# One product in 32 of the attention backward moved from VectorE to GpSimd by way of a ScalarE copy, and its group of units turned wholly by the DMA crossbar

## The chip, the cores and the metric

The kernel runs on one core of one Trainium2 chip. The metric is device time in microseconds. Before the change the median of three runs is 2561.26 us (2560.20 to 2564.32). The engines are TensorE (PE in the profile; its weight loads are PEld), VectorE (DVE), ScalarE (ACT), GpSimd (POOL) and SyncE (SP), which issues DMA. Matrix products land in PSUM, from which VectorE and ScalarE read.

## The reference

One transformer block (adaLN modulation, multi-head softmax attention, an MLP with squared ReLU) is computed forward and backward; the outputs are the block's result and the gradients of nine inputs. The sequence has S = 2048 tokens of width D = 512, with H = 32 heads of DH = 16. The change lies in the backward of the attention. For each head, with P the softmax probabilities, it computes

```
S  = Q K^T * scale            (2048 x 2048)
P  = exp(S), normalised       (the normalisation is folded into padded rows of V and dO)
dP = dO V^T - rowwise term    (2048 x 2048, one product of TensorE)
dS = P * dP                   (elementwise)
dV = P^T dO,  dK = dS^T Q,  dQ = dS K
```

The first four lines have 32 x 2048 x 2048 elements each, and the elementwise work on them is what occupies ScalarE (exp) and VectorE (P * dP).

## The kernel before, in words

The backward of the attention is `attn_bwd`. It loops over eight groups `g` of four heads, two head pairs `jp` in each, four chunks `c` of 512 keys, and sixteen blocks `ib` of 128 queries. One value of (g, jp, c, ib) is a **unit**: two heads `a`, 128 queries by 512 keys each. Four units in a row (`G = 4`, index `i`) are a **group**; a chunk has four groups. There are 1024 units, 256 groups and 64 chunks.

The order of instructions on every engine is the order in which the Python emits them; nothing reorders them. In each iteration, for each head `a`:

- PE computes the scores of this unit into an `st` tile (line 1555), and then `dP` of the *previous* unit into a `dp` tile (line 1494).
- ScalarE takes the exponential of the scores into `pu`, bf16 (line 1559).
- VectorE multiplies `dp` in PSUM by `pu` and writes `ds`, bf16 (line 1496). `ds` is one tile for the four units of a group.

`st` and `dp` come from rings of three PSUM buffers each (lines 1348 and 1349), `pu` from six buffers, `ds` from three, and the turned `dsT` from four. An instruction that writes a buffer waits until its reader of three tiles before is done.

After the two heads, work on older units follows on PE. In odd iterations `kv` (line 1448) multiplies `ds` and `pu` of two units, four and five units back, into the accumulator `acckv`; at the end of a chunk of keys (`ib` = 15) ScalarE copies `acckv` to `kvT` (line 1451). Since `kv` runs a group late, that copy falls into the last iteration of group 0 of the following chunk. In even iterations `dq` (line 1470) multiplies turned blocks of dS, `dsT`, by K.

`dsT` is made in two ways. In iteration 2 of a group, `turn_ds` has PE turn the four 128x128 blocks of the group's first product (i = 0, a = 0) into an `st` tile (line 1513), and ScalarE copies them into `dsT[:, 0:4]` (line 1514). The other 28 blocks are turned by one transposing DMA on SP's queue, issued in `dS` when the group's last unit is done (line 1504). `dq` reads `dsT` two groups later.

At the first and second group after the end of a head pair, `turn` (line 1459) has PE turn eight blocks of `kvT`, with two short copies by ScalarE to `dk_t` and `dv_t` (line 1463), and VectorE copies the accumulated dQ out (line 1477).

GpSimd's queue holds loads for the next head pair or group of heads. At the start of most groups it runs a one-element copy `tick` (line 1543), which waits for the first product of the group before, and then issues one DMA (line 1544).

`junk6` and `csq` are two f32 tiles of 128x512 in SBUF; the backward of the attention does not use them until its end.

Of the kernel before, what the change touches and what calls it, by code (L numbers as in the profile page):

```python
# [12 lines left out]
ALU = mybir.AluOpType  # L13
# [6 lines left out]
P = 128  # L20
# [85 lines left out]
class K:  # L106
# [1315 lines left out]
    def attn_bwd(self):  # L1422
# [7 lines left out]
        tc, nc = self.tc, self.nc  # L1430
        S, D, H, NQ, ST, SC = self.S, self.D, self.H, self.NQ, self.ST, self.SC
        G = 4
# [20 lines left out]
        def turn(g, jp, kvT, s0):  # L1453

            h0 = 4 * g + 2 * jp
            n = ST // 2
            tp = stp.tile([P, n, P], BF16, name="st")
            for st in range(n):
                nc.tensor.transpose(tp[:, st, :], kvT[:, (s0 + st) * P:(s0 + st + 1) * P], self.ident[:])
            v = tp[:].rearrange("p s (t a e) -> p t s a e", t=2, a=2)  # L1460
            for t, dst in enumerate((self.dk_t, self.dv_t)):
                d = dst[:, s0:s0 + n, h0 * DH:(h0 + 2) * DH].rearrange("p s (a d) -> p s a d", a=2)
                nc.scalar.copy(d, v[:, t, :, :, 0:DH])

        def dq(u, heads):
            (T, g, jp, c, ib, i, dsT) = u
            for a in heads:
                col = (2 * jp + a) * DH
                for sub in range(4):
                    nc.tensor.matmul(accq[:, ib, a, :], lhsT=dsT[:, (i * 2 + a) * 4 + sub, :],  # L1470
                                     rhs=T["K"][:, 4 * c + sub, col:col + DH],
                                     start=(c == 0 and ib == 0 and a == 0 and sub == 0), stop=False,
                                     skip_group_check=True)
            if c == SC - 1 and ib == ST - 1 and 1 in heads:
                h0 = 4 * g + 2 * jp
                d = self.dq_t[:, :, h0 * DH:(h0 + 2) * DH].rearrange("p s (a d) -> p s a d", a=2)
                nc.vector.tensor_scalar(d, accq[:], self.scale, None, ALU.mult)

        def kv_two(n=2):
            for u in pend[2 - n:2]:  # L1480
                kv(u)
            (T, g, jp, c, ib, kvT, pu, ds) = pend[1]
            del pend[:2]
            if c % 2 and ib == ST - 1 and (g, jp) == (NQ - 1, 1):
                turnq.append((g, jp, kvT, 4 * (c - 1)))
            elif c == SC - 1 and ib == ST - 1:
                turnq.extend((g, jp, kvT, s0) for s0 in (0, ST // 2))

        def dP(u, a):

            (T, g, jp, c, ib, kvT, pu, dsg, i, grp) = u
            rd = slice(64 - 64 * jp, 128 - 64 * jp)
            dp = dpp.tile([P, 512], F32, name="dp")
            nc.tensor.matmul(dp[:], lhsT=T["dOT"][rd, ib * P:(ib + 1) * P],  # L1494
                             rhs=masked["VT"][2 * jp + a][rd, 512 * c:512 * (c + 1)], start=True, stop=True)
            nc.vector.tensor_tensor(dsg[:, i, a], dp[:], pu[:, a, :], ALU.mult)  # L1496

        def dS(u):

            (T, g, jp, c, ib, kvT, pu, dsg, i, grp) = u  # L1500
            pend.append((T, g, jp, c, ib, kvT, pu, dsg[:, i]))
            if i == G - 1:
                dsT = grp[0]
                nc.sync.dma_start_transpose(dsT[:, 4:, :], dsg[:].rearrange("p i a k -> p (i a k)")[:, 512:])
                for i in range(G):
                    pendq.append((T, g, jp, c, ib - G + 1 + i, i, dsT))

        def turn_ds(dsg, grp):

            dsT = dtp.tile([P, 8 * G, P], BF16, name="dsT")  # L1510
            tp = stp.tile([P, 4, P], BF16, name="st")
            for b in range(4):
                nc.tensor.transpose(tp[:, b, :], dsg[:, 0, 0, b * P:(b + 1) * P], self.ident[:])  # L1513
            nc.scalar.copy(dsT[:, 0:4, :], tp[:])  # L1514
            grp.append(dsT)

        tick = self.tick
        T = self.T0
        turnq, last = [], None
        for g in range(NQ):  # L1520
            for jp in range(2):
                if jp == 0:
                    if g + 1 < NQ:
                        Tn, later = self.load_group(g + 1)
                    else:
                        Tn, later = None, self.wq_pieces(1) + self.load_wmt()
                    cut = len(later) // 2 if Tn else len(later)
                    pieces = self.pair_pieces(g, 1) + later[:cut]
                    later = later[cut:]
                elif g + 1 < NQ:  # L1530
                    pieces = self.pair_pieces(g + 1, 0) + later
                else:
                    pieces = [(self.xhat1_6[:, st, :], self.xhat1_d.rearrange("(st p) d -> p st d", p=P)[:, st, :])
                              for st in range(ST)]
                kvT = kvp.tile([P, S], BF16, name="kvT")
                total = len(pieces)
                for c in range(SC):
                    c0 = 512 * c
                    for ib0 in range(0, ST, G):
                        m = c * (ST // G) + ib0 // G  # L1540
                        while pieces and (total - len(pieces)) * SC * ST <= m * G * total:
                            if last:
                                nc.gpsimd.tensor_copy(tick[:], last[7][0:1, 0, 0, 0:1])  # L1543
                            nc.gpsimd.dma_start(*pieces.pop(0))
                        dsg, grp = self.dsp.tile([P, G, 2, 512], BF16, name="ds"), []
                        for i in range(G):
                            ib = ib0 + i
                            q = slice(ib * P, (ib + 1) * P)
                            if turnq and i == 2:
                                turn(*turnq.pop(0))  # L1550
                            pu = self.pup.tile([P, 2, 512], BF16, name="pu")
                            for a in range(2):
                                stt = stp.tile([P, 512], F32, name="st")
                                rs = slice(64 * jp, 64 * jp + 64)
                                nc.tensor.matmul(stt[:], lhsT=T["QT"][rs, q], rhs=masked["KT"][2 * jp + a][rs, c0:c0 + 512],  # L1555
                                                 start=True, stop=True)
                                if last:
                                    dP(last, a)
                                nc.scalar.activation(pu[:, a, :], stt[:], ACT.Exp, scale=self.scale)  # L1559
                            if last:  # L1560
                                dS(last)
                            last = (T, g, jp, c, ib, kvT, pu, dsg, i, grp)
                            if i % 2 == 1 and len(pend) >= 4:
                                kv_two()
                            elif i % 2 == 0 and len(pendq) > 2 * G:
                                for _ in range(4 if len(pendq) > 3 * G else 2):
                                    dq(pendq.pop(0), [0, 1])
                            if i == 2:
                                turn_ds(dsg, grp)
            T = Tn  # L1570
        with tc.manual_schedule(engines=ALL):
            for t in (2, 0):
# [338 lines left out]
```

The softmax here doesn't subtract the row's maximum and nothing guards it: scores larger than these inputs give would overflow.

## Time and profile before

| | |
|---|---|
| median of 3 runs | 2561.26 us |
| span of the profiled execution | 2562.0 us |
| its own time beside the span | no more than the span is shown for it; 0.7 us over the median |
| attention backward, first to last P * dP | 1180.6 to 2437.0 us |
| PE busy in the span | 2483.2 us (97%) |
| ScalarE busy | 2314.2 us (90%) |
| VectorE busy | 1767.4 us (69%), nearly all of the backward's stretch |
| GpSimd busy | 569.5 us (22%) |
| transposing DMAs of dS | 256, 6.7 us from issue to landing (median) |

How to read it: an engine's share is a mean over stages. Before 1180 us VectorE is busy two or three tenths, after it nine. A row of a group gives the busy time, the mean duration of one instruction in ns, and after the bar the idle time just before them with what ended it. Durations on ScalarE and VectorE overlap a little: the next instruction starts before the last one's recorded end, so the distance between starts is what one costs. Two heads' matmuls run beside each other on different rows of the array, so PE's records overlap too.

### The profile page before, as it was taken

Reading aid. Unit: us, or ns where it says so; the run is one execution under the profiler, and the core shown is the slowest. Engines: PE = TensorE matmul, PEld = TensorE weight load, DVE = VectorE, ACT = ScalarE, POOL = GpSimd, SP = SyncE. Lnnn points to the kernel's source line nnn. Section 1 sums busy time; section 2 is a strip of 40 time slices with the busy share of each in tenths; the row PEclk is TensorE's granted clock in tenths of the full one; section 3 lists DMA queues with packets and bytes.
Section 4 is the critical chain, followed back from the end, with each engine's and each line's share of the span. In section 5 each row is a group of like instructions: output and inputs, shape, how many; then the busy total and the mean of one; then the engine's idle time right before and its main releaser. Section 6 shows DMA issues by size and latency. Waiting matters only on the chain.

```text
span 2562.0 us, 77852 instructions
## 1 busy us (share of the span) xinstructions
PE 2483.2 (97%) x31239; PEld 1227.4 (48%) x31239; DVE 1767.4 (69%) x3651; ACT 2314.2 (90%) x3757; POOL 569.5 (22%) x1137
## 2 busy tenths in 40 slices
PE   8999899999999999899999999999999999999998
PEld 4555555555555554663444444444444444444443
DVE  6222323323322344667999999999999999999957
ACT  7999999999999996436999999999999999999935
POOL 3554521320221131353011111111111111111223
PEclk9999999999999999999999999999999999999999
DMA  4588742450351153799999999999999999999997
GB/s 165 118 180 196 173 95 83 100 113 22 112 128 49 39 143 113 154 190 211 205 205 202 199 200 201 203 204 200 197 199 198 208 201 197 201 201 229 213 202 191
DMA packets 1193040, 425.37 MB, mean 166 GB/s; under 512 B 1138004, under 2 KB 1161686, under 8 KB 1192678
## 3 DMA queue, kind: packets, MB, share of 16 engines
q1 hardware_dynamic: 1153542, 319.25, 64.2%
q0 software_dynamic: 37056, 100.11, 13.1%
q8 instruction: 244, 4.00, 0.6%
q10 hardware_dynamic: 2080, 1.05, 0.1%
q14 instruction: 118, 0.97, 0.1%
HBM read 73.73 MB, written 62.40 MB: 53 GB/s over the span
## 4 chain that ended last, share of the span: by engine, by line
PE 67%; ACT 20%; DMA 5%; issue 4%; POOL 2%; DVE 1%; SPq 1%; POOLq 0%; DVEq 0%; ACTq 0%
PE st L1555 20%; ACT pu L391 16%; PE acckv L1448 11%; PE accq L1470 8%; PE st L388 7%; PE accbank L322 3%; PE dp L1494 3%; ACT pu L1559 2%; PE st L1513 2%; PE dps L1047 2%; PE pps L1234 2%; PE dp L1604 1%; PE st L1699 1%; DMA dsT<-ds 1%; DMA ev_tm<-ev_fm 1%
## 5 line engine op out<-in xcount | busy, mean ns | idle before, releaser
L1496 DVE TENSOR_TENSOR ds<-dp,pu 128x512 bf16<-128x512 f32 x2048 | 1236.2, 679 | 13.1 <-PE dp L1494 10.2
L1559 ACT ACTIVATE pu<-st 128x512 bf16<-128x512 f32 x2048 | 1073.7, 612 | 46.4 <-PE dp L1494 22.5
L391 ACT ACTIVATE pu<-st 128x1024 bf16<-128x1024 f32 x992 | 912.1, 1077 | 4.6 <-PE st L388 4.4
L388 PE MATMUL st<-QTm,KTq 128*128 128x512 bf16 x1984 | 588.6, 377 | 19.5 <-ACT pu L391 6.0
L322 PEld LDWEIGHTS <-pu 128*128 128x128 bf16 x8192 | 347.5, 96 | 236.1 <-issue 3.1
L322 PE MATMUL accbank<-Vaug,pu 128*128 128x17 bf16 x8192 | 357.7, 171 | 1.2 <-ACT Vaug L522 0.9
L1494 PE MATMUL dp<-m,q 64*128 64x512 bf16 x1024 | 345.7, 382 | 1.1 <-DVE g2w L1053 0.7
L1494 PE MATMUL dp<-m,dOTg 64*128 64x512 bf16 x1024 | 344.6, 381 | 0.1
L1470 PEld LDWEIGHTS <-dsT 128*128 128x128 bf16 x8192 | 239.5, 96 | 213.8 <-issue 209.7
L1555 PE MATMUL st<-m,q 64*128 64x512 bf16 x1024 | 319.5, 382 | 9.2 <-ACT pu L1559 7.5
L1555 PE MATMUL st<-m,QTg 64*128 64x512 bf16 x1024 | 318.9, 381 | 9.5 <-ACT pu L1559 7.8
L388 PEld LDWEIGHTS <-KTq 128*128 128x128 bf16 x1984 | 188.3, 96 | 176.9 <-issue 125.5
L1543 POOL COPY tick<-ds 1x1 bf16<-1x1 bf16 x223 | 39.6, 178 | 1005.4 <-DVE ds L1496 1005.4
L1448 PE MATMUL acckv<-ds,q 128*16 128x512 bf16 x1024 | 154.0, 381 | 0.0
L1448 PE MATMUL acckv<-pu,dOg 128*16 128x512 bf16 x1024 | 154.0, 381 | 0.0
L1448 PE MATMUL acckv<-ds,Qg 128*16 128x512 bf16 x1024 | 154.0, 381 | 0.0
L1448 PE MATMUL acckv<-pu,q 128*16 128x512 bf16 x1024 | 154.0, 381 | 0.0
L1514 ACT COPY dsT<-st 128x512 bf16<-128x512 bf16 x256 | 152.4, 595 | 1.0 <-PE st L1513 1.0
L1470 PE MATMUL accq<-Kg,dsT 128*128 128x16 bf16 x4096 | 143.3, 170 | 3.4 <-DMA dsT<-ds 3.4
L1470 PE MATMUL accq<-q,dsT 128*128 128x16 bf16 x4096 | 143.6, 170 | 0.4 <-DMA dsT<-ds 0.3
L302 POOL DMA_DIRECT2D QTm<-QTq_d x124 | 63.3, 512 | 341.3 <-PE st L388 320.2
L329 DVE RECIPROCAL rl<-accbank 128x4 f32<-128x4 f32 x128 | 22.9, 179 | 162.6 <-PE accbank L322 162.5
(379 smaller groups left out, 2864.8 us busy)
## 6 DMA issues: line engine op xcount, KB each, us to landing
KTq<-KTq_d POOLq DMA_DIRECT2D x24, 512.0 KB, 3.9
duT_d<-auT POOLq DMA_DIRECT2D x3, 1792.0 KB, 7.8
aT_d<-rT POOLq DMA_DIRECT2D x3, 1792.0 KB, 11.1
KTq_d<-KTq SPq DMA_DIRECT2D x32, 128.0 KB, 2.0
QTq_d<-ev_fm SPq DMA_DIRECT2D x32, 128.0 KB, 3.9
VTq_d<-vT POOLq DMA_DIRECT2D x4, 1024.0 KB, 6.8
dsT<-ds SPq DMA_TRANSPOSE x256, 6.7
dx<-dx_d SPq DMA_DIRECT2D x16, 256.0 KB, 4.4
```

What stands on the lines that cost most here:

```text
L302: nc.gpsimd.dma_start(QTm[j][32 * j:32 * j + 32, :], self.QTq_d[g, 32 * j:32 * j + 32, 512 * qc:512 * (qc + 1)])
L322: nc.tensor.matmul(acc[:, a, sub, :], lhsT=pu[:, a, sub * P:(sub + 1) * P], rhs=Vaug[:, kb, h, :], start=(kb == 0 and a == 0 and sub == 0) ...
L388: nc.tensor.matmul(stt[:, a, :], lhsT=KT[:, kb * P:(kb + 1) * P], rhs=QTm[2 * jp + a][:], start=True, stop=True)
L391: nc.scalar.activation(pu[:], stt[:], ACT.Exp, scale=self.scale)
L1047: nc.tensor.matmul(pt[:], lhsT=a[st], rhs=g_tm[:, st, :], start=(st == 0), stop=(st == ST - 1))
L1448: nc.tensor.matmul(acckv[r:r + DH, :], lhsT=T[n][:, ib, col:col + DH], rhs=src[:, a, :], start=(ib == 0), stop=(ib == ST - 1))
L1470: nc.tensor.matmul(accq[:, ib, a, :], lhsT=dsT[:, (i * 2 + a) * 4 + sub, :], rhs=T["K"][:, 4 * c + sub, col:col + DH], start=(c == 0 and i ...
L1494: nc.tensor.matmul(dp[:], lhsT=T["dOT"][rd, ib * P:(ib + 1) * P], rhs=masked["VT"][2 * jp + a][rd, 512 * c:512 * (c + 1)], start=True, sto ...
L1496: nc.vector.tensor_tensor(dsg[:, i, a], dp[:], pu[:, a, :], ALU.mult)
L1514: nc.scalar.copy(dsT[:, 0:4, :], tp[:])
L1555: nc.tensor.matmul(stt[:], lhsT=T["QT"][rs, q], rhs=masked["KT"][2 * jp + a][rs, c0:c0 + 512], start=True, stop=True)
L1559: nc.scalar.activation(pu[:, a, :], stt[:], ACT.Exp, scale=self.scale)
```

## The change

In group 1 of every chunk (`off(c, ib)`: units 4 to 7), the dP tile of the group's first unit and second head is no longer multiplied by VectorE. ScalarE copies it from PSUM to `junk6` or `csq`, in turn, right after the exponential of the following unit's second head, and GpSimd multiplies the copy by `pu` and writes the same part of `ds`. In the same group `turn_ds` only allocates `dsT`; PE turns nothing, ScalarE copies nothing to `dsT`, and the transposing DMA takes all 32 blocks. That is 64 of 2048 tiles and 64 of 256 groups. The other groups are unchanged. (c * SC + ib // G) % 4 is ib // 4, since SC is 4.

```diff
             nc.tensor.matmul(dp[:], lhsT=T["dOT"][rd, ib * P:(ib + 1) * P],
                              rhs=masked["VT"][2 * jp + a][rd, 512 * c:512 * (c + 1)], start=True, stop=True)
+            if a == 1 and i == 0 and off(c, ib):
+                return dp
             nc.vector.tensor_tensor(dsg[:, i, a], dp[:], pu[:, a, :], ALU.mult)
+
+        def off(c, ib):
+            return (c * SC + ib // G) % 4 == 1
+
+        def dP_pool(u, dp):
+            (T, g, jp, c, ib, kvT, pu, dsg, i, grp) = u
+            f = (self.junk6, self.csq)[(c * SC + ib // G) // 4 % 2]
+            nc.scalar.copy(f[:], dp[:])
+            nc.gpsimd.tensor_tensor(dsg[:, i, 1], f[:], pu[:, 1, :], ALU.mult)
...
             if i == G - 1:
-                dsT = grp[0]
-                nc.sync.dma_start_transpose(dsT[:, 4:, :], dsg[:].rearrange("p i a k -> p (i a k)")[:, 512:])
+                dsT, n = grp
+                nc.sync.dma_start_transpose(dsT[:, n:, :], dsg[:].rearrange("p i a k -> p (i a k)")[:, n * P:])
...
-        def turn_ds(dsg, grp):
+        def turn_ds(dsg, grp, skip):
             dsT = dtp.tile([P, 8 * G, P], BF16, name="dsT")
+            grp.extend((dsT, 0 if skip else 4))
+            if skip:
+                return
             tp = stp.tile([P, 4, P], BF16, name="st")
             for b in range(4):
                 nc.tensor.transpose(tp[:, b, :], dsg[:, 0, 0, b * P:(b + 1) * P], self.ident[:])
             nc.scalar.copy(dsT[:, 0:4, :], tp[:])
-            grp.append(dsT)
...
-                                if last:
-                                    dP(last, a)
+                                held = dP(last, a) if last else None
                                 nc.scalar.activation(pu[:, a, :], stt[:], ACT.Exp, scale=self.scale)
+                                if held is not None:
+                                    dP_pool(last, held)
...
                             if i == 2:
-                                turn_ds(dsg, grp)
+                                turn_ds(dsg, grp, off(c, ib))
```

## The prediction

> **What bounds the kernel now.** I read the page's groups first, then the busy time by stage, then the timeline of one chunk, then single instructions on VectorE. The change touches only the attention backward, 1180 to 2437 us: 64 chunks (one per head pair and 512 keys) of four groups of four units. I write (n,a) for unit n of a chunk (0 to 15) and head a. The changed group is group 1, units 4 to 7: its product (4,1) moves, and its four turns on TensorE go.
>
> ```profile
> L1496 DVE TENSOR_TENSOR ds<-dp,pu 128x512 bf16<-128x512 f32 x2048 | 1236.2, 679 | 13.1 <-PE dp L1494 10.2
> L1559 ACT ACTIVATE pu<-st 128x512 bf16<-128x512 f32 x2048 | 1073.7, 612 | 46.4 <-PE dp L1494 22.5
> L1514 ACT COPY dsT<-st 128x512 bf16<-128x512 bf16 x256 | 152.4, 595 | 1.0 <-PE st L1513 1.0
> ```
>
> VectorE works 1236 of these 1257 us on one instruction, with 13 us idle in front of it. Its ends overlap: by single starts (1717.08, 1718.28 below, two apart) one costs 0.598 us of its queue, eight a group are 4.79 us. That looks like the bound. By stage:
>
> ```profile
> 1400.00:1700.00 300.00, 295.42 (x4214) 127.47 (x4213) 296.69 (x493) 292.60 (x582) 37.08 (x106) 1.00 1.02 201
> ```
>
> PE is busy 295, VectorE 297, ScalarE 293 of 300 us, GpSimd 37: three engines close together, so the order inside a chunk decides. Columns here are start, duration, engine:
>
> ```profile
> 1713.17 0.70 ACT L1451 ACTIVATE kvT<-acckv,kvs 128x512 bf16<-128x512 f32 x1
> 1713.74 3.07 ACT L1559 ACTIVATE pu<-st 128x512 bf16<-128x512 f32 x6
> ...
> 1714.41 0.37 PE L1555 MATMUL st<-m,QTg 64*128 64x512 bf16 x1 [0.25 <-ACT pu L1559]
> 1714.42 0.39 PE L1494 MATMUL dp<-m,dOTg 64*128 64x512 bf16 x1
> ...
> 1715.28 0.39 PE L1494 MATMUL dp<-m,dOTg 64*128 64x512 bf16 x1
> ...
> 1716.23 0.38 PE L1513 MATMUL st<-ident,ds 128*128 128x128 bf16 x4
> ...
> 1716.55 0.39 PE L1494 MATMUL dp<-m,dOTg 64*128 64x512 bf16 x1
> 1716.67 0.62 ACT L1514 COPY dsT<-st 128x512 bf16<-128x512 bf16 x1
> 1716.86 0.37 PE L1555 MATMUL st<-m,QTg 64*128 64x512 bf16 x1
> ...
> 1717.14 4.23 ACT L1559 ACTIVATE pu<-st 128x512 bf16<-128x512 f32 x8
> ...
> 1717.73 0.39 PE L1494 MATMUL dp<-m,dOTg 64*128 64x512 bf16 x1
> ```
>
> The reader is to see that this is group 1 and that it comes right behind the chunk's extra ScalarE work, the kvT copy: the six exponentials (4,0) to (6,1) start late, PE idles 0.25 us for one of them, and from there ScalarE has no gap. The dp rows shown are (4,1), (5,0), (6,0), (7,0). Now VectorE's products of (5,0), (6,0), (7,0), then (9,1), each asked for alone; and a case where VectorE really stood idle for its dp, with that dp:
>
> ```profile
> 1715.83 0.68 DVE L1496 TENSOR_TENSOR ds<-dp,pu 128x512 bf16<-128x512 f32 x1
> 1717.08 0.69 DVE L1496 TENSOR_TENSOR ds<-dp,pu 128x512 bf16<-128x512 f32 x1
> 1718.28 0.68 DVE L1496 TENSOR_TENSOR ds<-dp,pu 128x512 bf16<-128x512 f32 x1
> ...
> 1721.27 0.68 DVE L1496 TENSOR_TENSOR ds<-dp,pu 128x512 bf16<-128x512 f32 x1
> ```
> ```profile
> 1420.75 0.39 PE L1494 MATMUL dp<-m,dOTg 64*128 64x512 bf16 x1
> ...
> 1421.28 5.14 DVE L1496 TENSOR_TENSOR ds<-dp,pu 128x512 bf16<-128x512 f32 x8 [0.45 <-PE dp L1494]
> ```
>
> From dp's start to the product at the earliest is 0.53 us. In group 1 the distances are 0.55, 0.53 and 0.55: VectorE is "busy", but it has nothing waiting. At (9,1) the distance is 1.06 (dp 1720.21): there dp tiles wait, and VectorE sets the pace. So VectorE binds in groups 2, 3 and 0; in group 1 ScalarE and PE bind. The product that is removed lies in group 1. That is what my forecast rests on.
>
> **The change, part by part.**
>
> *Removed: one VectorE product per changed group.* 64 x 0.598 = 38.3 us of VectorE. It counts only if (5,0) can start earlier. Its dp starts at 1715.28, behind st(5,1), which waited for ScalarE (1714.41), so (5,0) starts at 1715.80 at best, 0.03 before now. The rest becomes idle VectorE.
>
> *Added and moved on ScalarE.* The copy of dp(4,1) to f stands behind exp (5,1) and ahead of exp (6,0); the dsT copy behind exp (6,1) goes. Copies of 128x512 f32 out of PSUM to f32 last 572 to 588 ns in the later stages, the dsT copy 595: the exchange is even, nine instructions before and after. Exponentials in this stretch follow each other by 0.48. Hence f starts at 1715.18 + 0.48 = 1715.66 (dp(4,1) is ready by 1714.9) and ends about 1716.25; exp (6,0) starts at 1716.13 instead of 1715.70, (6,1) at 1716.61, and (7,0), with no copy ahead of it, at 1717.09 (now 1717.14). Bounds for the slot of f: 0.45 (a 572 ns copy less the 0.12 of overlap) and 0.57 (the kvT copy, 1713.17 to 1713.74); I take 0.47 to 0.48, the dsT copy's. A buffer's next user starts 0.05 after its release (below, 1716.81 to 1716.86), so f frees dp(4,1)'s buffer at 1716.30, where VectorE freed it at 1715.96; dp(6,0) is the next user.
>
> *Removed on PE.* Four turns, 0.32 us from 1716.23 to the next st at 1716.55, and their st tile out of a ring of three. So st(7,0) goes at 1716.23, dp(6,0) at 1716.30 (now 1716.55). st(7,1) today waits for the end of exp (6,1), 1716.81 (hence 1716.86), because the turns' tile sits in the ring. Then it waits for exp (6,0), which f has pushed to end at 1716.74: st(7,1) at 1716.79. The gain on the path is 0.07 us. Behind it stand kv and dp(7,0), now at 1717.73, then 1717.66: earliest product 1718.19. VectorE's own queue: (5,0) 1715.80 and four more by 0.598 gives (7,0) at 1718.19. Both say 0.09 sooner than 1718.28. PE works without a gap to (9,1), which waits for VectorE again: the 0.09 is kept, no more is added, and what is late next is again ScalarE in the next group 1.
>
> *Chunks that open a head pair* (15 of the 64) carry eight kvT turns and two ScalarE copies in group 1, and VectorE idles there already (0.45 us, shown). The timeline from 1417 to 1426 shows a ScalarE hole of 0.1 us before those copies and a spacing of 0.27 between them, so f pushes exp (6,0) by 0.23 only, to 1421.62, end 1422.23. st(7,1) goes at 1422.28 instead of 1422.54; PE is gapless from there to the product (9,0), which idles 0.19 us for dp today. Gain 0.26.
>
> *Added on GpSimd.* One product of f by P, 64 times. Nearest rows: f32 by f32 1283 ns, bf16 by bf16 1163. It runs 1716.4 to 1717.7. It is first read by kv of unit 4, four units later, at 1719.32: 1.6 us of cover, and the transposing DMA is later still. Behind it in the queue stands the next group's tick and load, now at 1715.45, then about 1717.7; the loads are for the next head pair or the next group of heads and one head pair (16 of them in 1257 us, so 79 us) spreads 12 to 16 of them, so nobody waits. Exp (10,0), six units on, reuses P's buffer, at 1720.28. Cost nothing; if the cover were gone, each us beyond 1.6 would stop PE 64 times.
>
> The Trainium skill (GPSIMD Engine Reference, 4.1 Engine selection) speaks against this move: elementwise work belongs on VectorE, GpSimd being about twice as slow for two inputs. The rows agree on the ratio (1.16 to 1.28 against 0.68 us); charged to the path the rule would add some 64 x 0.6 = 38 us, an estimate, charged to a cover of 1.6 us nothing.
>
> *Moved: four blocks to the crossbar.*
>
> ```profile
> L1504 SPq DMA_TRANSPOSE dsT<-ds x256: 3370/3624/6962, 1185.6 to 2440.0; - x128
> ```
>
> 28 blocks take 3.62 us of SP's queue, so 32 take 4.14, of a group of at least 4.2 (seven products). Landing takes 6.7 us, then about 7.2; dq reads the tile two groups (9.5 us) after the issue, and VectorE rewrites ds sixteen products (9.6) after. Cost nothing. The DMA engines rest about 0.9 us of each group now (half-us stretches from 1700.5 show 0.12 and 0.00 of their share), which covers the 0.5.
>
> *Sum.* 49 x 0.08 + 15 x 0.26 = 3.9 + 3.9 = 7.8 us (0.08 between the 0.07 and 0.09 above). The profiled execution's span is 2562.0, 0.7 above the median of 2561.26: 2554.2 against its own time, 2553.5 against the median. About 0.2% (5.1 us) is what can be told from no change. With f at 0.45 the ordinary chunk gains 0.11, sum 9.3; with 0.57 it loses 0.02, and the sum is 2.9.
>
> **Rivals.**
>
> *VectorE binds throughout:* each removed product counts whole, 38.3 us, 2523. For it: 99% busy. Against it: the distances 0.55, 0.53, 0.55. In part it holds if ScalarE reaches group 1 earlier than I think: half of it is 2542.
>
> *Nothing moves:* f needs 0.57 or its extra waits eat 0.1 us; 2557 to 2563. For it: a margin of only 0.07 at st(7,1). Against: the short f32 copies.
>
> *Slower: GpSimd holds VectorE up.* A VectorE operation with both inputs in SBUF, L1078, has a median of 692 ns and twice went to about 2 us while a GpSimd product ran. If ds suffered so, VectorE would lose about 1.28 us per changed group, of which 0.6 was freed: 64 x 0.7 = 45 us, 2606. It decides as soon as ds beside GpSimd takes over 1.2 us. Against it: the first two ds ran beside this POOL row, and the worst of the first sixteen is 691 ns:
>
> ```profile
> 1180.28 1.28 POOL L1054 TENSOR_TENSOR dgb_acc<-dgb_acc,g2w 128x512 f32<-128x512 f32 x1
> 1180.61 4.87 DVE L1496 TENSOR_TENSOR ds<-dp,pu 128x512 bf16<-128x512 f32 x8
> ```
>
> **How the numbers follow.** Forecast case (gain 4 to 11) 0.50, of which 0.40 lies beyond 0.2%; a larger gain 0.10; nothing 0.25, of which 0.07 a loss just over 0.2%; clearly slower (GpSimd against VectorE, kv late, crossbar backed up) 0.15. Faster 0.50, same 0.28, slower 0.22. The range leaves out the upper half of the larger gains and most of the slower case: 2540 to 2568.
>
> **What would show it.** ds on VectorE at 1984 instructions, some 1198 us busy, and its idle time up by about 30 us, released by dp and lying at (5,0). Nearly no shorter spacing of groups 2, 3 and 0. exp (6,0) behind f, st(7,1) released by it. The GpSimd product near 1.2 us with no kv waiting for it. SP's transposes at two durations, 3.6 and 4.1. I am wrong if VectorE's idle time stays at 13 us (then the first rival holds), if ds gets longer, or if PE waits for GpSimd or for dsT.

## The result, and the profile after

The changed kernel takes 2551.96 us (median of 20 runs), the one before 2559.29 us (median of 20, the first three shown ahead included). The ratio is 0.9973 with a 95% interval of 0.9965 to 0.9981: by the ratio 6.9 us faster, between 4.9 and 9.0 (the medians lie 7.3 apart). The forecast was 7.8 us.

The row of the product on VectorE and of the reads of `dsT` on PE, from the page of the changed kernel:

```profile
L1498 DVE TENSOR_TENSOR ds<-dp,pu 128x512 bf16<-128x512 f32 x1984 | 1200.5, 679 | 44.4 <-PE dp L1494 25.3
L1470 PE MATMUL accq<-Kg,dsT 128*128 128x16 bf16 x4096 | 143.3, 170 | 3.2 <-DMA dsT<-ds 3.1
```

VectorE lost 36 us of work and gained 31 us of idle time in front of the same instruction. Nearly all that was taken off it came back as waiting: 39.4 of the 44.4 us lie at (5,0), where 7.2 us lay before. The profile puts 25.3 us down to `dp` and 16.8 us to ScalarE's copy f; those 16.8 lie in 16 chunks, nearly all of which open a head pair, but in every one of them the product starts 0.52 to 0.53 us after its dp, the shortest distance of before, so there too it is dp that it waits for. How the waiting comes about, the timeline of group 1 of an ordinary chunk shows (start, duration, engine; lines of the older units left out):

```profile
1783.08 0.70 ACT L1451 ACTIVATE kvT<-acckv,kvs 128x512 bf16<-128x512 f32 x1
1783.65 2.09 ACT L1571 ACTIVATE pu<-st 128x512 bf16<-128x512 f32 x4
...
1784.32 0.37 PE L1568 MATMUL st<-m,QTg 64*128 64x512 bf16 x1 [0.26 <-ACT pu L1571]
1784.33 0.39 PE L1494 MATMUL dp<-m,dOTg 64*128 64x512 bf16 x1
...
1785.19 0.39 PE L1494 MATMUL dp<-m,dOTg 64*128 64x512 bf16 x1
...
1785.56 0.66 ACT L1506 COPY csq<-dp 128x512 f32<-128x512 f32 x1
1785.71 4.93 DVE L1498 TENSOR_TENSOR ds<-dp,pu 128x512 bf16<-128x512 f32 x8 [0.50 <-PE dp L1494]
1786.03 4.15 ACT L1571 ACTIVATE pu<-st 128x512 bf16<-128x512 f32 x8
...
1786.27 0.37 PE L1494 MATMUL dp<-m,dOTg 64*128 64x512 bf16 x1
1786.30 1.15 POOL L1507 TENSOR_TENSOR ds<-csq,pu 128x512 bf16<-128x512 f32 x1 [4.75 <-ACT csq L1506]
1786.77 0.37 PE L1568 MATMUL st<-m,QTg 64*128 64x512 bf16 x1
...
1787.64 0.39 PE L1494 MATMUL dp<-m,dOTg 64*128 64x512 bf16 x1
```

Count from the start of exp (4,0), 1783.65 here and 1713.74 before. (The rows that start 0.01 us apart on PE, 1784.32 and 1784.33, are the scores of one unit and dP of the unit before it, for the same head; these are the two that run beside each other.) dp(5,0) comes at 1.54 in both, and VectorE, without its product (4,1), stands idle 0.50 us for it. The copy f starts at 1.91. exp (6,0) moves from 1.96 to 2.38, as worked out ahead. dp(6,0) comes sooner, 2.62 instead of 2.81. But st(7,1) comes at 3.12 in both, and dp(7,0) at 3.99 in both, within 0.01. That line is where the gain of an ordinary chunk should have been.

The distance between two kvT copies is the length of a chunk. In the trace of the change an ordinary one is 19.17 to 19.18 us (19.19 before, 1693.98 to 1713.17), and one that opens a head pair 20.60 (20.81 before):

```profile
1920.51 0.70 ACT L1451 ACTIVATE kvT<-acckv,kvs 128x512 bf16<-128x512 f32 x1
...
1939.69 0.70 ACT L1451 ACTIVATE kvT<-acckv,kvs 128x512 bf16<-128x512 f32 x1
```

Over the backward that makes 49 x 0.02 + 15 x 0.21 = 4.1 us. From the first product to the last one the two profiled executions differ by 4.4 us (1257.1 and 1252.7). The spans, 2562.0 and 2548.2, differ by more; the rest lies before and behind the backward, where both kernels have the same instructions.

### The profile page after: what moved, and what is told of

It is laid out like the page before. It is cut to its first block, busy times and chain, and to the rows that moved or that the text cites. A ratio compares the mean times of both kernels' runs of the same rounds, so it can differ in the third digit from the quotient of the medians.

```text
span 2548.2 us, 77305 instructions
## 1 busy us (share of the span) xinstructions
PE 2468.2 (97%) x30983; PEld 1216.0 (48%) x30983; DVE 1730.1 (68%) x3587; ACT 2310.2 (91%) x3757; POOL 637.3 (25%) x1201
## 3 DMA queue, kind: packets, MB, share of 16 engines
q10 hardware_dynamic: 2080, 1.05, 0.1%
## 4 chain that ended last, share of the span: by engine, by line
PE 62%; ACT 27%; issue 5%; DMA 3%; DVE 2%; POOL 1%; DVEq 0%; ACTq 0%; POOLq 0%
ACT pu L391 18%; PE st L1568 17%; PE acckv L1448 9%; PE st L388 8%; PE accq L1470 7%; ACT pu L1571 7%; PE accbank L322 3%; PE dp L1494 2%; PE dps L1047 2%; PE st L1527 2%; PE pps L1234 2%; PE dp L1618 1%; DMA dsT<-ds 1%; PE pps L631 1%; PE st L1713 1%
## 5 line engine op out<-in xcount | busy, mean ns | idle before, releaser
L1498 DVE TENSOR_TENSOR ds<-dp,pu 128x512 bf16<-128x512 f32 x1984 | 1200.5, 679 | 44.4 <-PE dp L1494 25.3
L1556 POOL COPY tick<-ds 1x1 bf16<-1x1 bf16 x223 | 39.4, 177 | 510.5 <-DVE ds L1498 510.5
L1568 PEld LDWEIGHTS <-q 64*128 64x128 bf16 x1024 | 58.9, 94 | 121.4 <-issue 104.8
```

## The experiments

The theory to test: VectorE binds in groups 2, 3 and 0 only; in group 1 ScalarE and PE bind, so what gains is PE and ScalarE being spared the turns, and the product that left VectorE gains nothing. The main rival: VectorE binds throughout.

**The product alone.** GpSimd gets the product, PE and ScalarE keep the turns.

```diff
-                                turn_ds(dsg, grp, off(c, ib))
+                                turn_ds(dsg, grp, False)
```

> The product (4,1) goes to GpSimd by way of f as in the change, but PE and ScalarE still turn the group's first four blocks, so ScalarE has ten instructions in group 1 instead of nine. Theory (ScalarE and PE bind in group 1, VectorE only in groups 2, 3 and 0): exp (6,1) ends about 0.45 us later, st(7,1) behind it too, and each changed group costs about 0.45 us: 64 x 0.45 = 29 us slower than before, ratio 1.011. VectorE's idle time rises by well over 38 us. Rival (VectorE binds throughout, its removed product is the gain): 38 us faster, ratio 0.985.

Measured: 2580.32 us against 2559.31, ratio 1.0087 (1.0069 to 1.0105). By the ratio the kernel becomes slower by 22 us although VectorE has 64 products less. An ordinary chunk is 19.67 us, 0.48 more than before: one ScalarE instruction. One that opens a head pair is 21.09 us, 0.28 more; the 29 us expected had 0.45 for every chunk and were somewhat too much.

```profile
1857.88 0.70 ACT L1451 ACTIVATE kvT<-acckv,kvs 128x512 bf16<-128x512 f32 x1
...
1877.55 0.70 ACT L1451 ACTIVATE kvT<-acckv,kvs 128x512 bf16<-128x512 f32 x1
```

The rival falls by sign. In group 1 of an ordinary chunk a ScalarE instruction has its full price, and the VectorE product that was taken off did not make up for any of it.

**The crossbar alone.** VectorE keeps all products; group 1 is turned wholly by the crossbar.

```diff
-            if a == 1 and i == 0 and off(c, ib):
+            if False:
```

> VectorE keeps all its products; only the turning of group 1 goes wholly to the crossbar, so PE loses four turns and ScalarE one copy there. Theory: exp (6,0) isn't pushed back, st(7,1) goes 0.3 to 0.4 us earlier than before, and VectorE's own queue limits what is won: 0.06 us in an ordinary chunk, 0.5 us in the 15 that open a head pair (there VectorE idles today): 48 x 0.06 + 15 x 0.5 = 10 us faster than before, ratio 0.996, at least as fast as the change. Rival (the product taken off VectorE is what gained): no gain, ratio 1.000.

Measured: 2552.73 us, ratio 0.9971 (0.9955 to 0.9987), the same as the change with everything (0.9973). An ordinary chunk is 19.13 us, one that opens a head pair 20.55 (0.26 gained where I expected 0.5).

```profile
1839.56 0.70 ACT L1451 ACTIVATE kvT<-acckv,kvs 128x512 bf16<-128x512 f32 x1
...
1840.13 6.33 ACT L1571 ACTIVATE pu<-st 128x512 bf16<-128x512 f32 x12
...
1842.92 0.38 PE L1568 MATMUL st<-m,q 64*128 64x512 bf16 x1
...
1843.80 0.39 PE L1494 MATMUL dp<-m,q 64*128 64x512 bf16 x1
```

Without f in the way st(7,1) comes at 2.79 after exp (4,0) instead of 3.12, and dp(7,0) at 3.67 instead of 3.99: the 0.3 us that f had eaten. VectorE then sets the pace, and of the 0.3 us only 0.06 reaches the length of the chunk.

**The product left out.** As the change, without f and the GpSimd product.

```diff
-            nc.scalar.copy(f[:], dp[:])
-            nc.gpsimd.tensor_tensor(dsg[:, i, 1], f[:], pu[:, 1, :], ALU.mult)
+            nc.gpsimd.memset(dsg[:, i, 1], 0.0)
```

> As the change, but f and the GpSimd product are left out: GpSimd sets that part of ds to zero instead, so dS of one tile in 32 is missing from dQ and dK. Beside the crossbar-only run it prices the product on VectorE, beside the change it prices f and the GpSimd product. Theory: 48 x 0.09 + 15 x 0.53 = 12 us faster than before, ratio 0.995: 2 us better than crossbar only (the product in group 1 is worth next to nothing), 5 us or more better than the change (f pushes two exponentials back). Rival (VectorE binds): 38 us faster, ratio 0.985.

Measured: 2548.94 us, ratio 0.9957 (0.9937 to 0.9978). An ordinary chunk is 19.12 us, one that opens a head pair 20.55:

```profile
1840.42 0.70 ACT L1451 ACTIVATE kvT<-acckv,kvs 128x512 bf16<-128x512 f32 x1
...
1859.54 0.70 ACT L1451 ACTIVATE kvT<-acckv,kvs 128x512 bf16<-128x512 f32 x1
```

Beside the crossbar alone (19.13), 64 products of 0.598 us that nobody carries out any more are worth 0.01 us a chunk. The intervals of the two ratios overlap. So the product's place on VectorE in group 1 is worth nothing that can be told.

**Another place.** The same change in group 3, where `dp` tiles wait for VectorE.

```diff
-            return (c * SC + ib // G) % 4 == 1
+            return (c * SC + ib // G) % 4 == 3
```

> The same change, made in group 3 of each chunk instead of group 1. Theory: in group 3 dp tiles do wait for VectorE (distances 0.62 to 1.06), so the removed product counts until (13,0) meets its dp: 0.29 us a chunk, and ScalarE has 0.15 us of idle time there to take f: 64 x 0.29 = 19 us faster than before, ratio 0.993. Rival (the place doesn't matter, the gain of the change is what a freed ScalarE and PE slot is worth anywhere): 4 to 8 us, ratio 0.997 to 0.998. Rival (VectorE binds throughout): 38 us.

Measured: 2547.40 us, ratio 0.9949 (0.9933 to 0.9966), 13 us. An ordinary chunk is 18.92 us, 0.27 less than before.

```profile
1838.20 0.70 ACT L1451 ACTIVATE kvT<-acckv,kvs 128x512 bf16<-128x512 f32 x1
...
1857.12 0.70 ACT L1451 ACTIVATE kvT<-acckv,kvs 128x512 bf16<-128x512 f32 x1
```
```profile
1868.74 0.59 ACT L1506 COPY csq<-dp 128x512 f32<-128x512 f32 x1
...
1869.12 3.10 DVE L1498 TENSOR_TENSOR ds<-dp,pu 128x512 bf16<-128x512 f32 x5 [0.23 <-PE dp L1494]
```

Here VectorE's idle time after the missing product is 0.23 us, not 0.50. An idle time counts from the recorded end, and two products without a gap overlap by 0.08, so 0.31 of the 0.598 us is lost here and 0.29 won; in group 1 it was 0.58 and 0.02. The place decides. (That it is the product and not the four spared turns of group 3 is seen below, in the run with the crossbar everywhere: there group 3 is spared its turns as well, VectorE keeps the product, and an undisturbed chunk is 19.13 us, no shorter than with group 1 alone turned by the crossbar.) The gain over all is less than 64 x 0.29: chunks that open a head pair gain 0.26, and some chunks are longer than 18.92. Some of that is waiting for the crossbar, for PE waits 5.1 us for `dsT` between 1200 and 2400 us here, against 0.6 before.

**A control.** The changed kernel with `== 4` for `== 1`, so that the condition is never true.

> A control: the changed kernel with its condition never true, so that every engine gets the instructions of before in the same order. In the traces the backward is 4.5 us shorter with the change (1257.1 to 1252.7), but the runs say 6.9; the crossbar-only and group 3 runs also gained about 2 us more than their backward shows. Theory: those 2 us are spread between programs or chance, and this run shows a ratio of 1.000 within its interval, with an ordinary chunk of 19.19 us. Rival: something outside the tested lines became faster by 2 to 3 us, ratio 0.999.

Measured: 2560.09 us, ratio 1.0008 (0.9993 to 1.0024); an ordinary chunk 19.19 us. The interval is 4 us wide to either side, so the 2 us by which the runs beat the traces are within what it leaves open. One trace leaves more open still: in the control's, the backward takes 1262.3 us, 5.2 more than before with the same instructions, nearly all of it in one chunk of 24.34 us; and its backward begins at 1171.1 us where that of before begins at 1180.6. A difference of 2 us can't be told from one profiled execution of each kernel, and it is not explained further.

**The crossbar everywhere.** VectorE keeps its products, no group is turned by PE.

```diff
-            if a == 1 and i == 0 and off(c, ib):
+            if False:
...
-                                turn_ds(dsg, grp, off(c, ib))
+                                turn_ds(dsg, grp, True)
```

> VectorE keeps all products, and the crossbar turns all 32 blocks in every group, not only in group 1. Theory: with group 1 relieved, VectorE's 32 products a chunk (32 x 0.598 = 19.1 us) bind everywhere, so relieving the other groups too adds nothing: as crossbar only, ordinary chunk 19.13, ratio 0.996 to 0.998. The crossbar keeps up (4.1 us of SP's queue in 4.8). Rival (the crossbar is near its limit): dq waits for dsT, and the kernel is slower than before, ratio above 1.005.

Measured: 2587.24 us, ratio 1.0111 (1.0092 to 1.0131). My theory was wrong, the rival right. The waits for `dsT` between 1200 and 2400 us in this run (us in all, times, the longest):

```profile
PEld L1470 <- DMA dsT<-ds: 123.1, 137, 4.9
...
PE accq L1470 <- DMA dsT<-ds: 40.7, 50, 4.2
```

and the transposing DMAs on SP's queue (minimum, median, maximum in ns):

```profile
L1515 SPq DMA_TRANSPOSE dsT<-ds x256: 3924/4372/6922, 1181.2 to 2464.8; - x128
```

Undisturbed chunks are 19.13 us as expected, but many are one or two us longer. The two rows of waits are not to be added: nearly the whole of PE's idle time for `dsT` lies inside that of the weight loads (PEld), which wait while earlier matmuls still run. What counts is PE's own row, 41 us against 0.6 before. By as much the chunks grew: what 61 of them (all but the first and the last two) are longer than the shortest of their kind adds up to 40 us here, and to 1.5 us before.

I had multiplied 28 blocks' 3.62 us up to 4.14. In the change, where one group in four has 32 blocks, these take 4.07 us in the median; here, where every group has them, the median is 4.37 and the mean 4.64 of 4.78 us, and landings go up to 11.6 us (8.8 before). The queue is nearly full: 109 of the 256 transpositions start within 0.15 us of the end of the one before, against 9 before, so a late one has hardly anything to catch up in. Why 32 blocks take longer here than in the change is open. The Trainium skill (DMA: Bandwidth & Descriptors, Latency and other measured facts) gives 261 GB/s for a transposition in its unfavourable case. By that figure 32 blocks of 32 KB, 1.05 MB, need 4.0 us, an estimate, and should pass in 4.78. The queue took 4.64 in the mean and PE waited, so the measurement decides.

**The crossbar everywhere, the product moved in groups 2 and 3.**

```diff
-            return (c * SC + ib // G) % 4 == 1
+            return (c * SC + ib // G) % 4 in (2, 3)
...
-            f = (self.junk6, self.csq)[(c * SC + ib // G) // 4 % 2]
+            f = (self.junk6, self.csq)[(c * SC + ib // G) % 2]
...
-                                turn_ds(dsg, grp, off(c, ib))
+                                turn_ds(dsg, grp, True)
```

> The crossbar turns everything in every group, and the product (i = 0, a = 1) of groups 2 and 3 goes to GpSimd by way of f. Theory: VectorE binds there, and each moved product is worth about 0.3 us as in the group 3 run: 64 x (2 x 0.3 + 0.06) = 42 us faster than before, ratio 0.984, ordinary chunk 18.5 us. Rival (ScalarE's two extra copies take the slot of the turns and set the pace): at most the 13 us of the group 3 run, ratio 0.995. Rival (crossbar): as above, the shorter group leaves 4.1 us of SP's queue in 4.5, and dq waits.

Measured: 2571.93 us, ratio 1.0043 (1.0027 to 1.006). Slower than before, not the 42 us faster of the theory. The undisturbed chunks of its trace are 18.58 us, near the 18.5 expected, and most are longer, with PE waiting for `dsT`: the crossbar again. (The trace is of the longest of the twelve executions, 2597.76 us, so the size of its waits is not used.)

**Three products for one.** The change with the GpSimd product issued three times.

```diff
-            nc.gpsimd.tensor_tensor(dsg[:, i, 1], f[:], pu[:, 1, :], ALU.mult)
+            for _ in range(3):
+                nc.gpsimd.tensor_tensor(dsg[:, i, 1], f[:], pu[:, 1, :], ALU.mult)
```

> The change with the GpSimd product issued three times over. One product ends 3.81 us after exp (4,0) starts and kv of unit 4 comes at 5.58 (trace of the change), so the cover is 1.77 us; two more take 2.3. Theory: kv waits about 0.5 us for GpSimd in each changed group, and since some dp tiles wait for VectorE by then, 0.2 to 0.5 us of it reach the end: 13 to 32 us slower than the change, ratio to before 1.002 to 1.010. VectorE's products keep 0.68 us each. Rival (GpSimd holds VectorE up): VectorE's products beside GpSimd get longer and the loss is above 60 us. Rival (kv isn't the reader that matters): no loss, 0.997.

Measured: 2585.56 us, ratio 1.0111 (1.0092 to 1.013), 28 us more than before and some 35 more than the change, by the ratios; an ordinary chunk 19.74 us, 0.57 more than the change.

```profile
1783.70 4.93 DVE L1498 TENSOR_TENSOR ds<-dp,pu 128x512 bf16<-128x512 f32 x8 [0.49 <-PE dp L1494]
1784.29 3.63 POOL L1508 TENSOR_TENSOR ds<-junk,pu 128x512 bf16<-128x512 f32 x3 [9.54 <-ACT junk L1506]
...
1787.97 0.38 PE L1448 MATMUL acckv<-ds,Qg 128*16 128x512 bf16 x1 [0.39 <-POOL ds L1508]
...
1788.51 0.39 PE L1569 MATMUL st<-m,QTg 64*128 64x512 bf16 x1
...
1788.98 1.08 ACT L1572 ACTIVATE pu<-st 128x512 bf16<-128x512 f32 x2 [0.82 <-POOL tick L1557]
```

The eight products of VectorE take 4.93 us beside 3.63 us of GpSimd work, as they do beside 1.15: GpSimd doesn't hold VectorE up. `kv` waits for GpSimd, as the cover of 1.77 us says. The exponential after it, (10,0), waits longer, 0.82 us. The profile puts that down to a GpSimd `tick`, but the third product had ended 1.06 us earlier, at 1787.92, so it isn't the buffer of P that holds the exponential up. Its scores start only at 1788.51, on PE behind the late `kv`, and it follows them by 0.47 us, just as in the trace of the change (1789.75 and 1790.22): the wait is the wait of `kv`, passed on. The loss is a little above the range expected.

**Both places.** Groups 1 and 3 turned wholly by the crossbar, the product moved in group 3 only.

```diff
-            return (c * SC + ib // G) % 4 == 1
+            return (c * SC + ib // G) % 4 == 3
...
-                                turn_ds(dsg, grp, off(c, ib))
+                                turn_ds(dsg, grp, ib // G in (1, 3))
```

> The crossbar turns all of dS in groups 1 and 3, the product goes to GpSimd in group 3 only. In the traces crossbar only took an ordinary chunk from 19.19 to 19.13 us and one that opens a head pair from 20.81 to 20.55, the group 3 version to 18.92 and 20.55. Theory (each part is worth what its own group's binding engine leaves, and they add): 18.86 and 20.29, 48 x 0.33 + 15 x 0.52 = 24 us faster than before, ratio 0.991. Rival (the crossbar, which could not take 32 blocks in every group, is late with 32 in every second one too): dq waits for dsT, ratio above 0.995.

Measured: 2549.18 us, ratio 0.9953 (0.9935 to 0.9971), no better than group 3 alone. The theory is met chunk by chunk and the rival in the sum:

```profile
1896.35 0.70 ACT L1451 ACTIVATE kvT<-acckv,kvs 128x512 bf16<-128x512 f32 x1
...
1915.21 0.70 ACT L1451 ACTIVATE kvT<-acckv,kvs 128x512 bf16<-128x512 f32 x1
```
```profile
PEld L1470 <- DMA dsT<-ds: 41.4, 54, 2.4
...
PE accq L1470 <- DMA dsT<-ds: 16.7, 25, 2.0
```

Undisturbed chunks are 18.86 and 20.29 us, as added up ahead, but many are longer, by 17 us in all, and PE waits 16.7 us for `dsT`.

**Three places.** Groups 1, 2 and 3 turned by the crossbar, the product moved in groups 2 and 3; f alternates by group as above.

```diff
-            return (c * SC + ib // G) % 4 == 1
+            return (c * SC + ib // G) % 4 in (2, 3)
...
-                                turn_ds(dsg, grp, off(c, ib))
+                                turn_ds(dsg, grp, ib // G in (1, 2, 3))
```

> The crossbar turns all of dS in groups 1, 2 and 3, the product goes to GpSimd in groups 2 and 3. Theory (the backing up in the run with 32 blocks in every group is an average limit: 4.37 us of SP's queue a group, plus the loads): with 31 blocks a group on average and a shorter group (18.6 us a chunk, 4.64 a group) the crossbar is late again, PE waits more than 20 us for dsT, and the ratio is between 0.995 and 1.003. Rival (31 are few enough): ordinary chunk 18.6 us, 64 x 0.6 = 38 us faster than before, ratio 0.985.

Measured: 2545.40 us against 2563.09, ratio 0.9942 (0.9920 to 0.9964), a little better than the range I gave for a late crossbar, far from the rival's 0.985.

```profile
1894.36 0.70 ACT L1451 ACTIVATE kvT<-acckv,kvs 128x512 bf16<-128x512 f32 x1
...
1912.94 0.70 ACT L1451 ACTIVATE kvT<-acckv,kvs 128x512 bf16<-128x512 f32 x1
```

Undisturbed chunks are 18.58 us; the longer ones are so by 25 us in all, and PE waits 25.2 us for `dsT`, as the theory had it (more than 20). This version is faster than both kernels. So is the group 3 version by its ratio, 0.9949 against 0.9973, but its interval just touches that of the change. The intervals of these two versions overlap, so which is the better one is open.

## Why the prediction was right

**What binds.** Right. The step that the forecast rested on, that the distances of 0.55, 0.53 and 0.55 mean a VectorE with nothing waiting in group 1, is shown by three runs: the product alone is slower (1.0087), the crossbar alone gains as much as the change (0.9971), the product left out adds 0.01 us a chunk. The 38.3 us of VectorE counted for nothing, as said.

**VectorE.** 1984 products, 1200.5 us busy (1198 said), idle 44.4 us (about 30 more said, 31 found), nearly all of it at (5,0).

**ScalarE.** The order and the start of exp (6,0) were right, 2.39 after exp (4,0) said and 2.38 found. Two sizes were not. f lasts 655 ns where I had rows of 572 to 588, but keeps its slot of 0.47. And exp (6,0), which now starts on the heels of f, is recorded with 0.69 us instead of the 0.61 that I added to its start:

```profile
1786.03 0.69 ACT L1571 ACTIVATE pu<-st 128x512 bf16<-128x512 f32 x1
```

Its end, which st(7,1) waits for, therefore lies where the end of exp (6,1) lay before.

**PE.** The mis-sized term of the sum is "the gain on the path is 0.07 us" at st(7,1), and the 0.09 from it: it measured 0.00 at st(7,1) and 0.02 in the chunk. The same term made 0.26 into 0.21 in the chunks that open a head pair; there exp (6,0) lasts 0.72. So with the terms as measured the sum is about 4 us, a little below the measured interval (4.9 to 9.0), while the forecast of 7.8 lies inside it. As far as the record shows, that the mis-sized sum came nearer to 6.9 than the right one is luck. The mechanism doesn't rest on it, for the chunk lengths and the three runs above show it. What stands between 4.1 and 6.9 us is open: the control leaves room for 4 us either way.

**GpSimd.** The product takes 1.15 us and nothing waits for it; the tripled product puts the limit of its cover where it was said. The slower rival is excluded by the durations of all products on VectorE in the changed kernel:

```profile
L1498 DVE TENSOR_TENSOR ds<-dp,pu x1984: 670/679/693, 1173.5 to 2425.5; 128x512 bf16<-128x512 f32 x199
```

**Crossbar.** "Cost nothing" nearly held for 29 blocks a group on average (PE waits 1.1 us for `dsT` between 1200 and 2400, against 0.6), and the two durations are there: 3.62 us in the median in the other groups and 4.07 in group 1 (3.6 and 4.1 said). But its reason, a queue with 0.6 us to spare in every group, was too light: with 30 blocks a group PE waits 16.7 us, and 32 make the kernel slower.

## What to carry to other kernels

A busy share near 100% does not make an engine the bound: look, instruction by instruction, at the distance between an operand's start and its use, and compare it with the shortest distance that the trace shows; only where it is longer is there a queue that a removed instruction can shorten. When work is taken off one engine by way of another, the copy's slot on that other engine has its price where it stands in the order, and the same edit two groups later was worth about twice as much (13 us against 6.9; in the traces' backward 10.8 against 4.4). For instructions that follow each other without a gap, count from end to end (0.48 to 0.50 us here), not from a start plus the duration of one that had waited.

## What was not expected of the hardware

The record of a ScalarE exponential of 128x512 grows along a train of instructions that follow each other at once: from 0.62 to 0.65 us in the four behind the kvT copy, in both kernels, and on to 0.69 to 0.72 in the four behind f, with starts still 0.48 to 0.49 apart; later in the same chunks it is 0.59 to 0.62. A transposing DMA of 32 blocks takes 4.07 us of SP's queue in the median when one group in four has one, and 4.37 when every group has, where 28 blocks take 3.62: the price of the last four blocks was not fixed, and it rose as the queue filled.
